# Row sums loaded, inverted and sent over three quads, and a third quad with five sum terms

## The chip, the cores and the metric

The kernel runs on one core of one Trainium2 chip. A core has a matrix engine (TensorE, PE in the profile; PEld is its weight load), a vector engine (VectorE, DVE), an activation engine (ScalarE, ACT), GpSimd (POOL) and SyncE (SP), which here issues nearly all DMA transfers. Each engine takes its own instructions in order and waits for semaphores. The metric is the device time of one execution in microseconds (us); the median of the runs is compared. A profile shows one execution: its span runs from the first to the last instruction.

## What is computed

Attention with normalised queries and keys, and then a feed-forward block whose activation is a softmax times its own input:

```python
# q, k, v: (8, 12, 448, 64)
q_n, k_n = rmsnorm(q, g_q), rmsnorm(k, g_k)
attn = softmax(q_n @ k_n.T / sqrt(64))          # rows divided by their sum
x = (attn @ v) -> (8 * 448, 12 * 64)            # 3584 tokens of 768
h = x @ w_in                                    # 768 -> 1024
solu = h * softmax(h)
out = layer_norm(solu) * g_ln @ w_out           # 1024 -> 768
```

The kernel doesn't divide the attention weights. It forms the exponentials, multiplies them by v, sums the exponentials of each row apart, and multiplies the result by the inverse of the sum only when the feed-forward block takes x in.

## The kernel before

**Stages.** The attention runs over 24 quads, numbered 0 to 23; a quad is four heads of one batch, so three quads make a batch of twelve heads. In the profile it takes the first 306.6 us. Then the feed-forward block runs in two stages, and PE works through them to the end at 789.4 us.

**A quad.** Quads 2 to 23 have one shape. The loop over m (lines 1573 to 1746) writes the order of all engines out by hand. The 448 keys are cut into seven groups (0 to 6) of 64. For each group PE forms the scores (`both_scores`, line 885), ScalarE takes the exponential into a tile E (line 845), and PE multiplies E by v into `o` (`both_values`, line 897). PE's order in a quad is scores 0, 1, 2, 3, values 0, scores 4, values 1, scores 5, values 2, scores 6, values 3 to 6. `o` is one PSUM tile with one buffer. `take` (line 1000, VectorE) copies it to `xo`, and values 0 of the next quad can't start before that copy has ended. The store of `xo` to DRAM is SP's (line 1009).

**Row sums.** The exponentials of a row are summed on PE by matmuls with a tile of ones (`sums`, line 962). To have fewer such matmuls, VectorE first adds E tiles in pairs: `add_pair` (line 905) makes a term of two tiles, `add_to` (line 911) adds a third to a term, `join_terms` (line 915) makes one of two terms. `quads[m]["terms"]` lists what the sums of quad m go over, in this order, with E6 put in front. A quad of `two_terms` ends with two terms, other late quads with three, quads 1 and 2 with four. The sums of three quads are formed together at the end of quads 2, 5, 8, 11, 14, 17, 20 and 23 (`sums_at`), 8 matmuls for each term.

**What becomes of the sums.** In the quad after, ScalarE copies them out of PSUM (`keep_sums`, lines 974 and 976) and SP sends them to DRAM (`sd`, line 979). Then, for batch b: `load_sums` (line 988) loads the batch's sums from DRAM spread over 128 partitions, 42 on each, into the tile `inv`, which has one buffer; `invert` (line 992) is VectorE's reciprocal; `send_inverses` (line 995) sends the inverses to DRAM (`rd`), from where the feed-forward stage loads them (`load_r`, line 1049) and multiplies x by them (`scale`, line 1062). The dictionary `inverts_at` (line 1471) says when: at its key m, SP loads at the start of quad m, VectorE inverts in the middle of the same quad, and SP sends at the start of quad m+1. Batch 7 is handled later, in the feed-forward stage.

**VectorE's order in a quad** (from quad 6 on): the take of the quad before, with the two or three short steps of the norm (lines 724 to 729) before or behind it; two row reductions of squares (line 696); two transposes of queries and keys (line 756), which wait for `qkn` from GpSimd (line 735); the reciprocal, where there is one; two pair adds, two further adds, the join, and in quads of `steps_at` two operations of the weight conversion (lines 545 and 546).

**SP's order in a quad:** load v (line 675), two stores of x (line 1009, behind the take), sums to DRAM, inverses to DRAM, load of sums, a load of weights (line 513), and the pieces of q and k (line 647, eight a quad from quad 6 on, ten before that), which ScalarE squares a quad and more later (line 690).

Of the kernel before, what the change touches and what calls it, by code (L numbers as in the profile page):

```python
# [366 lines left out]
def fast_path(  # L367
# [24 lines left out]
    nc = tc.nc  # L392
    B, H, S, D = q.shape
# [6 lines left out]
    NQ = B * NP // 2  # L400
# [225 lines left out]
    quads = {}  # L626
# [275 lines left out]
    def add_pair(m, x, y):  # L902
        d = quads[m]
        e = work.tile([P, 2, S], FP32, tag="es", name="es", bufs=6)
        nc.vector.tensor_tensor(e, d["E", x], d["E", y], OP.add)  # L905
        d.setdefault("terms", []).append((2, e))

    def add_to(m, k, x, engine):
        d = quads[m]
        e = d["terms"][k][1]  # L910
        engine.tensor_tensor(e, e, d["E", x], OP.add)  # L911
# [82 lines left out]
    def send_inverses(b):  # L994
        nc.sync.dma_start(rd[b].rearrange("j r c -> (j r c)").rearrange("(p x) -> p x", p=P), inverses[b])

    def take(m):
        d = quads[m]
        d["xo"] = work.tile([P, 2, S], FP32, tag="xo", name="xo", bufs=1)
        nc.vector.tensor_copy(d["xo"], d["o"][:, :, 0:S])  # L1000
        for i in range(2):
            del st[2 * m + i]
# [465 lines left out]
    combines_at[23] = (10, 11)  # L1468
    two_terms = (3, 4, 6, 7, 9, 10, 12, 13, 15, 16, 18, 19, 22)
    sums_at = (2, 5) + tuple(range(8, NQ, 3))  # L1470
    inverts_at = {4: (0,), 8: (1,), 10: (2,), 14: (3,), 16: (4,), 20: (5,), 22: (6,)}
    wq += [(moe_w_out, c + k, i) for c in range(HF) for k in (0, HF) for i in range(2)]
    again = [(w, w.shape[0] // P, i) for w in (moe_w_in, moe_w_out) for i in range(-(-w.shape[0] // P * w.shape[1] // S))]
    extent = consts.tile([P, len(again)], FP32, name="extent")
# [29 lines left out]
    with tc.manual_schedule():  # L1504
# [68 lines left out]
        for m in range(1, NQ):  # L1573
            a, b = 2 * m, 2 * m + 1
            next1 = m + 1 < NQ
            next2 = m + 2 < NQ
            early = EARLY <= m
            four = m < 3

            def score(x):  # L1580
                unit(lambda: both_scores(m, x))

            def value(x):
                unit(lambda: both_values(m, x))

            if m == 3:
                norm_gain()
            sent = None
            if kept:
                sent = keep_sums(*kept)  # L1590
                kept = None
            if next1:
                load_v(m + 1)
            beside = combines_at.get(m, ())
            if beside:
                if m - 1 in steps_at:
                    step = wq[steps_at.index(m - 1)]
                    pass_on(w_in[(0, 3, 1, 2)[step[1] // HD * 2 + step[2]]][0:1, step[1] % HD, 0:1])
                else:
                    pass_on(quads[m - 1]["terms"][-1][1][0:1, 0, 0:1])  # L1600
                for x in beside:
                    combine_in(x)
                take(m - 1)
            if early and next1:
                rsqrt_step(norms[m + 1])
            if m > 1 and not beside:
                take(m - 1)
            store_x(m - 1)
            if sent:
                sent()  # L1610
            for x in inverts_at.get(m - 1, ()):
                send_inverses(x)
            for x in inverts_at.get(m, ()):
                load_sums(x)
            if early and m + 2 in steps_at:
                load_next()
            if m == 1:
                score(0)
                score(1)
                score(2)  # L1620
                rsqrt_seed(norms[2])
                rsqrt_step(norms[2])
                normalise(4)
                normalise(5)
                load_pieces(8)
                score(3)
                squares(6)
                row_sums(6)
                qk_transpose(4)
                value(0)  # L1630
                score(4)
                squares(7)
                qk_transpose(5)
                row_sums(7)
                value(1)
                score(5)
                fold_sums(3)
                value(2)
                score(6)
                gains(2)  # L1640
            else:
                if m == 2:
                    add_pair(1, 0, 1)
                    add_to(1, 1, 2, nc.vector)
                    score(0)
                    rsqrt_seed(norms[3])
                if next1:
                    if not early:
                        rsqrt_step(norms[m + 1])
                    if m == 2:  # L1650
                        add_pair(1, 3, 4)
                        quads[1]["terms"].append((2, quads[1]["E", 5]))
                    normalise(a + 2)
                    normalise(b + 2)
                    if m == 22:
                        combine_in(9)
                if early:
                    load_pieces(2)
                else:
                    load_pieces(10)  # L1660
                    if m + 2 in steps_at:
                        load_next()
                if early and next2:
                    row_sums(a + 4)
                    row_sums(b + 4)
                    load_pieces(6)
                if m == NQ - 1:
                    scale(0)
                if m != 2:
                    score(0)  # L1670
                if m > 2 and not early:
                    squares(a + 4)
                    row_sums(a + 4)
                score(1)
                if next1:
                    qk_transpose(a + 2)
                if m > 2 and not early:
                    squares(b + 4)
                    row_sums(b + 4)
                if m == 2:  # L1680
                    score(2)
                    squares(a + 4)
                    row_sums(a + 4)
                    score(3)
                    squares(b + 4)
                    row_sums(b + 4)
                    qk_transpose(b + 2)
                else:
                    if next1:
                        qk_transpose(b + 2)  # L1690
                    for x in inverts_at.get(m, ()):
                        invert(x)
                    score(2)
                    score(3)
                if next2:
                    fold_sums(m + 2)
                value(0)
                score(4)
                if m in steps_at:
                    low_bits, join, product = convert_w(wq[steps_at.index(m)], raws[steps_at.index(m)])  # L1700
                    low_bits[0]()
                value(1)
                score(5)
                if m in steps_at:
                    low_bits[1]()
                if next1 and early and m not in sums_at:
                    gains(m + 1)
                add_pair(m, 0, 1)
                if four:
                    add_to(m, 0, 2, nc.vector)  # L1710
                    add_pair(m, 3, 4)
                else:
                    add_pair(m, 2, 3)
                    add_to(m, 0, 4, nc.vector)
                    add_to(m, 1, 5, nc.vector)
                    if m in two_terms:
                        join_terms(m)
                value(2)
                score(6)
                if next1 and (not early or m in sums_at):  # L1720
                    gains(m + 1)
                if m in steps_at:
                    join()
                if next2:
                    rsqrt_seed(norms[m + 2], m not in steps_at or m + 1 in steps_at)
                if m + 1 >= EARLY and m + 3 < NQ:
                    squares(a + 6)
                    squares(b + 6)
                if four:
                    quads[m]["terms"].append((2, quads[m]["E", 5]))  # L1730
            quads[m].setdefault("terms", []).insert(0, (2, quads[m]["E", NK - 1]))
            if m == NQ - 2:
                load_x(0)
                load_r(0)
            if m == NQ - 1:
                load_x(1)
                sizes(0)
                block_sums(0, 0)
                block_sums(0, 1)
            for x in range(3, NK):  # L1740
                value(x)
            waiting.append(m)
            if m in sums_at:
                unit(lambda: None)
                kept = end_sums()
                waiting.clear()
        take(NQ - 1)
        sent = keep_sums(*kept)
        store_x(NQ - 1)
# [185 lines left out]
```

## Time and profile before

| | |
|---|---|
| runs | 791.09 us median of 3 (790.87 to 793.43) |
| the profiled execution | 791.04 us, span 789.4 us |
| granted TensorE clock | 0.997 |
| PE, PEld busy | 769.7 us (97%), 473.1 us (60%) |
| DVE, ACT, POOL busy | 610.2 us (77%), 511.8 us (65%), 483.3 us (61%) |
| DMA | 134.27 MB, mean 170 GB/s |
| end of the attention's sums on PE | 306.55 us |

Busy time is the union of an engine's instructions; a matmul's end is modelled, so a busy PE is not a PE at its peak. In a row of the timeline the first two numbers are the start (us from the span's start) and the length of one or several like instructions; the bracket at its end is the idle time of that engine just before it and what ended it. In a row of waits stand the waiting instruction, what it waited for, the us in total, how often, and the longest. In a row of windows stand the window, its length, the busy time of each engine with its instructions in brackets (PE, PEld, DVE, ACT, POOL), the clock, the mean busy share of the 16 DMA engines and GB/s. The length of a row can overlap the start of the next, since an engine begins an instruction before the last has been acknowledged.

### The profile page before, as it was taken

What the parts mean: (1) busy time and instruction counts of PE and PEld (TensorE: products, weight loads), DVE (VectorE), ACT (ScalarE), POOL (GpSimd) and SP (SyncE); (2) the same over time, 40 slices, a digit from 0 to 9 for tenths busy, and PEclk for the clock granted to TensorE, in tenths of its full rate; (3) what the DMA queues carried; (4) which work ended last, traced back from release to release, by engine and by line L of the source; (5) the groups of instructions that cost most, each with busy time, mean ns of one, the idle gap of its engine ahead of it and who ended that gap; (6) DMA issues with size and microseconds to landing.
All of it is one profiled execution on the core that took longest, in us unless ns stands there. A gap on an engine that the chain in (4) does not pass through costs nothing.

```text
span 789.4 us, 14850 instructions
## 1 busy us (share of the span) xinstructions
PE 769.7 (97%) x5158; PEld 473.1 (60%) x5158; DVE 610.2 (77%) x1038; ACT 511.8 (65%) x847; POOL 483.3 (61%) x635
## 2 busy tenths in 40 slices
PE   8999998999999999999999999999999999999996
PEld 4444444444444444444444444444899999999996
DVE  6779989998999886677788667676697695776844
ACT  6778997878888873687777656556626445464410
POOL 2464443453544544454587688888898777777851
PEclk9999999999999999999999999999999999999998
DMA  9999999999999546677887777773757647457212
GB/s 161 180 178 198 192 202 159 202 183 171 182 181 187 127 129 155 162 182 174 197 186 168 165 156 168 160 184 75 216 157 248 201 147 253 149 179 249 99 55 86
DMA packets 279818, 134.27 MB, mean 170 GB/s; under 512 B 190324, under 2 KB 264884, under 8 KB 279732
## 3 DMA queue, kind: packets, MB, share of 16 engines
q1 hardware_dynamic: 265892, 123.31, 69.9%
q10 hardware_dynamic: 13840, 9.90, 4.3%
q8 instruction: 43, 0.70, 0.4%
q14 instruction: 43, 0.35, 0.2%
HBM read 96.12 MB, written 37.04 MB: 169 GB/s over the span
## 4 chain that ended last, share of the span: by engine, by line
PE 72%; DVE 10%; SPq 5%; issue 5%; DMA 4%; POOL 3%; ACT 1%; DVEq 0%
PE A L1340 16%; PE A L1114 14%; PE B L1114 9%; PE B L1340 8%; PE D L1114 5%; PE C L1114 5%; PE o L897 4%; PE C L1340 4%; SPq L647 4%; PE s L885 4%; POOL qkn L735 3%; DVE xo L1000 2%; DVE es L905 2%; DVE qkT L756 2%; DVE es L911 2%
## 5 line engine op out<-in xcount | busy, mean ns | idle before, releaser
L845 ACT ACTIVATE E<-s 128x896 f32<-128x896 f32 x144 | 124.4, 920 | 27.7 <-PE s L885 26.9
L885 PE MATMUL s<-qkT 64*64 64x448 f32 x1288 | 138.8, 540 | 0.0
L897 PE MATMUL o<-E,v 64*64 64x448 f32 x1104 | 120.8, 538 | 6.4 <-DVE xo L1000 6.4
L735 POOL TENSOR_TENSOR qkn<-qk,ny 128x896 f32<-128x896 f32 x45 | 77.1, 1735 | 74.5 <-DVE ny L729 42.0
L885 PEld LDWEIGHTS s<-qkT 64*64 64x64 f32 x1288 | 66.0, 190 | 59.2 <-issue 37.5
L897 PEld LDWEIGHTS o<-E,v 64*64 64x64 f32 x1104 | 41.1, 133 | 65.8 <-issue 45.1
L1340 PE MATMUL A<-w_out,sums 128*128 128x192 f32 x392 | 79.7, 326 | 0.0
L1340 PE MATMUL B<-w_out,sums 128*128 128x192 f32 x392 | 79.7, 326 | 0.0
L1114 PE MATMUL A<-w_in,xg 128*128 128x512 f32 x168 | 76.8, 593 | 0.0
L1114 PE MATMUL B<-w_in,xsum 128*128 128x512 f32 x168 | 76.7, 592 | 0.0
L1340 PEld LDWEIGHTS B<-w_out,sums 128*128 128x128 f32 x392 | 66.3, 190 | 0.0
L1340 PEld LDWEIGHTS A<-w_out,sums 128*128 128x128 f32 x392 | 66.3, 190 | 0.0
L756 DVE STREAM_TRANSPOSE qkT<-qkn 128x896 f32<-128x896 f32 x46 | 49.9, 1099 | 9.9 <-POOL qkn L735 9.9
L1114 PEld LDWEIGHTS B<-w_in,xsum 128*128 128x128 f32 x168 | 31.9, 190 | 40.2 <-issue 39.7
L1114 PEld LDWEIGHTS A<-w_in,xg 128*128 128x128 f32 x168 | 31.8, 190 | 40.1 <-issue 38.9
L1216 ACT ACTIVATE u<-u,shift,he 128x1024 f32<-128x1024 f32 x28 | 34.8, 1242 | 28.2 <-POOL shift L1212 28.1
L696 DVE TENSOR_REDUCE part<-sq 128x28 f32<-128x896 f32 x46 | 47.9, 1074 | 4.3 <-ACT sq L690 4.3
L905 DVE TENSOR_TENSOR es<-E 128x896 f32<-128x896 f32 x46 | 49.0, 1101 | 0.0
L1090 POOL TENSOR_TENSOR xsum<-xg 128x384 f32<-128x384 f32 x14 | 14.4, 1030 | 55.7 <-ACT xsum L1073 38.7
L911 DVE TENSOR_TENSOR es<-es,E 128x896 f32<-128x896 f32 x44 | 47.7, 1123 | 0.1
L1340 PE MATMUL A<-w_out,s 128*128 128x192 f32 x224 | 45.6, 326 | 0.0
L690 ACT ACTIVATE sq<-qk 128x896 f32<-128x896 f32 x45 | 41.0, 944 | 1.8 <-issue 0.6
(175 smaller groups left out, 1655.8 us busy)
## 6 DMA issues: line engine op xcount, KB each, us to landing
ur<-ud SPq DMA_DIRECT2D x60, 256.0 KB, 4.5
ud<-ub SPq DMA_DIRECT2D x112, 128.0 KB, 2.9
xd<-xo SPq DMA_DIRECT2D x48, 224.0 KB, 3.8
qk<-in_q_dram SPq DMA_DIRECT2D x92, 112.0 KB, 4.5
qk<-in_k_dram SPq DMA_DIRECT2D x92, 112.0 KB, 4.0
v<-in_v_dram SPq DMA_DIRECT2D x23, 448.0 KB, 5.2
out_dram<-P SPq DMA_DIRECT2D x19, 384.0 KB, 3.8
raw<-in_moe_w_in_dram SPq DMA_DIRECT2D x12, 512.0 KB, 5.4
```

Source lines behind the costliest of these rows:

```text
L690: nc.scalar.activation(d["sq"].rearrange("p (s b) d -> p s (b d)", s=2), d["qk"], AF.Square)
L696: nc.vector.tensor_reduce(norms[m]["part"][:, i], st[n]["sq"], AX, OP.add)
L735: e.tensor_tensor(d["qkn"].rearrange("p (s b) d -> p s b d", s=2), d["qk"].rearrange("p s (b d) -> p s b d", d=32), y.rearrange("p (s b) - ...
L756: nc.vector.transpose(d["qkT"].rearrange("p s t -> p (s t)"), d["qkn"].rearrange("p b d -> p (b d)"))
L845: nc.scalar.activation(e, s[:, :, 0:S], AF.Exp)
L885: nc.tensor.matmul(s[i * D : (i + 1) * D, h, 0:S], qkT[hh, i, 1, keys], qkT[hh, i, 0], start=True, stop=True)
L897: nc.tensor.matmul(d["o"][h * D : (h + 1) * D, i, 0:S], d["v"][pp, h, kc], d["E", kc][pp, h], start=kc == 0, stop=kc == NK - 1,)
L905: nc.vector.tensor_tensor(e, d["E", x], d["E", y], OP.add)
L911: engine.tensor_tensor(e, e, d["E", x], OP.add)
L1114: nc.tensor.matmul(k[bank], a[:, c], w_in[i][:, c], start=begin and c == 0, stop=c == HD - 1, skip_group_check=not begin,)
L1216: nc.scalar.activation(d["u"], d["u"], AF.Identity, scale=d["e"], bias=d["shift"])
L1340: nc.tensor.matmul(k[bank], a[:, c].rearrange("p a i -> p (a i)"), w_out[:, area, i, c], start=begin and c == 0, stop=c == KC - 1, skip_gr ...
```

## The change

Four edits. The table `inverts_at` becomes regular: batch x is loaded at the start of quad 4+3x (4, 7, 10, 13, 16, 19, 22 in place of 4, 8, 10, 14, 16, 20, 22). VectorE inverts it one quad after the load, in quad 5+3x, and SP sends the inverses at the start of quad 6+3x; for batch 6 that is behind the last quad. So each of the three steps has a quad of its own, and the reciprocals now stand in quads 5, 8, 11, 14, 17, 20 and 23.

In quad 2 (index 2, the third) E2 is no longer added to the first pair. The terms become E6, E5, E2, E0+E1, E3+E4 in this order, five in place of four (E6, E0+E1+E2, E3+E4, E5).

The third item of the change's title, two terms in the fifth quad, has no line in the diff: `two_terms` holds index 4 before and after.

```diff
-    inverts_at = {4: (0,), 8: (1,), 10: (2,), 14: (3,), 16: (4,), 20: (5,), 22: (6,)}
+    inverts_at = {4 + 3 * x: (x,) for x in range(B - 1)}
...
-            for x in inverts_at.get(m - 1, ()):
+            for x in inverts_at.get(m - 2, ()):
                 send_inverses(x)
             for x in inverts_at.get(m, ()):
                 load_sums(x)
...
-                    for x in inverts_at.get(m, ()):
+                    for x in inverts_at.get(m - 1, ()):
                         invert(x)
                     score(2)
                     score(3)
...
                 add_pair(m, 0, 1)
                 if four:
-                    add_to(m, 0, 2, nc.vector)
                     add_pair(m, 3, 4)
+                    quads[m]["terms"] = [(2, quads[m]["E", x]) for x in (5, 2)] + quads[m]["terms"]
...
-                if four:
-                    quads[m]["terms"].append((2, quads[m]["E", 5]))
             quads[m].setdefault("terms", []).insert(0, (2, quads[m]["E", NK - 1]))
...
+        for x in inverts_at.get(NQ - 2, ()):
+            send_inverses(x)
         take(NQ - 1)
```

## The prediction

> **What bounds the kernel now.** I read the page first, then the waits of TensorE (PE) and VectorE (DVE), then the rows of the tile `inv`, then the time of each quad from one `take` to the next. From the page:
>
> ```profile
> span 789.4 us, 14850 instructions
> PE 769.7 (97%) x5158; PEld 473.1 (60%) x5158; DVE 610.2 (77%) x1038; ACT 511.8 (65%) x847; POOL 483.3 (61%) x635
> ```
>
> PE looks full, but 19.7 us of the span are not, and the waits from quad 8 to quad 23 (110.6 to 295.8 us) all name DVE first; the waits of DVE over the same quads follow:
>
> ```profile
> PE o L897 <- DVE xo L1000: 5.9, 7, 1.5
> PE sm L962 <- DVE es L911: 2.9, 5, 1.2
> ...
> DVE inv L992 <- DMA inv<-sd: 8.6, 5, 3.7
> DVE qkT L756 <- POOL qkn L735: 6.0, 10, 1.8
> ```
>
> The same view names no wait of PE after 300 us, so whatever attention saves reaches the end. The tile `inv` holds the row sums; its load, and three of the five waits in DVE's timeline (start, us, instruction, idle before):
>
> ```profile
> L988 SPq DMA_DIRECT2D inv<-sd x8: 422/682/1317, 65.5 to 317.6; - x8
> ...
> 118.24 0.42 DVE L992 RECIPROCAL inv<-inv 128x42 f32<-128x42 f32 x1 [3.68 <-DMA inv<-sd]
> ...
> 142.40 0.42 DVE L992 RECIPROCAL inv<-inv 128x42 f32<-128x42 f32 x1 [1.03 <-DMA inv<-sd]
> ...
> 265.18 0.42 DVE L992 RECIPROCAL inv<-inv 128x42 f32<-128x42 f32 x1 [1.25 <-DMA inv<-sd]
> ```
>
> The reader is to see an instruction of 0.42 us that holds up its whole engine for a load issued in the same quad. Is DVE idle time worth anything? Windows from one take to the next, quads 8 to 13, and the whole of quads 8 to 22 (length, then PE, PEld, DVE, ACT, POOL busy):
>
> ```profile
> 109.48:124.22 14.74, 13.11 (x164) 5.98 (x160) 10.99 (x15) 10.65 (x17) 4.55 (x7) 1.00 1.06 190
> 124.22:136.29 12.07, 12.07 (x132) 5.77 (x132) 11.93 (x16) 11.51 (x16) 4.55 (x7) 1.00 0.84 150
> 136.29:147.80 11.51, 11.07 (x120) 4.98 (x112) 10.45 (x12) 9.87 (x15) 4.55 (x7) 1.00 1.01 203
> 147.80:159.61 11.81, 11.05 (x146) 5.22 (x144) 11.28 (x14) 8.91 (x14) 6.79 (x9) 1.00 1.08 185
> ...
> 109.48:294.57 185.09, 176.33 (x1972) 82.73 (x1968) 169.15 (x203) 151.78 (x215) 85.86 (x119) 1.00 0.89 171
> ```
>
> Against them the start of the first `values` matmul of a quad, which needs the take before it, and the start of the sums of quad 8, from PE's timeline:
>
> ```profile
> 110.71 0.93 PE L897 MATMUL o<-E,v 64*64 64x448 f32 x8
> 118.34 0.59 PE L962 MATMUL sm<-El,ones 128*32 128x224 f32 x8
> ...
> 148.94 0.98 PE L897 MATMUL o<-E,v 64*64 64x448 f32 x8 [0.76 <-DVE xo L1000]
> 162.52 0.93 PE L897 MATMUL o<-E,v 64*64 64x448 f32 x8
> ...
> 273.22 0.93 PE L897 MATMUL o<-E,v 64*64 64x448 f32 x8
> 283.75 0.95 PE L897 MATMUL o<-E,v 64*64 64x448 f32 x8
> 295.71 0.98 PE L897 MATMUL o<-E,v 64*64 64x448 f32 x8 [0.50 <-DVE xo L1000]
> ```
>
> Four constants come out. PE undisturbed takes 283.75-273.22 = **10.53** per quad, and 162.52-148.94 = **13.58** in a quad that ends with sums. The first value follows a take's start by at least 148.94-147.80 = **1.14**. The values end 118.34-110.71 = **7.63** after the first. From 110.71 to 295.71 PE needs 10 x 10.53 + 5 x 13.58 = 173.2 of 185.0 us: 11.8 idle. DVE over the same quads has 185.09 us, of which 8.6 are the wait for `inv`: 176.5 left. So **DVE paces these quads**, PE is 3.3 us behind it as second, and DVE's wait is worth nearly its length.
>
> **The change, part by part.** (1) Loads move from quads 8, 14, 20 to 7, 13, 19; inverses to 5, 8, 11, 14, 17, 20, 23 (before: 4, 8, 10, 14, 16, 20, 22); sends to 6, 9, 12, 15, 18, 21 and behind the last quad. Every inverse now stands a whole quad, 10 us and more, behind its load; the longest of the five waits is 3.7, so all 8.6 us should go. Behind the waiting reciprocal stood es adds, the join, the weight conversion and the take, and PE waited for the adds (2.9) and the takes (5.9).
>
> What is late next? I walk the quads, with take(m) the later of DVE's own work and the values' end. Quad 8: DVE needs 14.74-3.68 = 11.06, take(8) at 120.54; first value of 9 at 110.71+13.58 = 124.29 (PE, above 121.68). Quad 9: 12.07 more, take(9) at 132.61; values end 131.92, so no wait. First value of 10: 134.82 by PE, 133.75 by DVE. Quad 10: 11.51 less its wait of 1.03 and less a reciprocal, 0.34 (0.42 less the 0.08 by which the end of one row overlaps the start of the next, as at 47.58+1.09 and 48.59 below): 10.14, take(10) at 142.75; values end 142.45. Margin 0.3, the least of all. Quad 11: 11.81+0.34, take(11) at 154.90. Further on DVE leads nowhere but lags, so its sum holds: 185.09-8.6-0.34 (six reciprocals become five) = 176.1, still above PE's 173.2. **Gain of this part: 9.0 us.** Its bounds: 11.8 if PE alone counted; 2.9 if only PE's waits at the sums went and the takes stayed late.
>
> (2) Quad 2 adds one term to the sums and drops one DVE add. DVE and PE there, and DVE's next wait:
>
> ```profile
> 47.58 1.09 DVE L911 TENSOR_TENSOR es<-es,E 128x896 f32<-128x896 f32 x1
> 48.59 1.19 DVE L905 TENSOR_TENSOR es<-E 128x896 f32<-128x896 f32 x1
> 53.78 1.08 DVE L696 TENSOR_REDUCE part<-sq 128x28 f32<-128x896 f32 x1 [2.63 <-ACT sq L690]
> ...
> 49.83 0.59 PE L962 MATMUL sm<-es,ones 128*32 128x224 f32 x8 [0.52 <-DVE es L905]
> 50.24 0.56 PE L962 MATMUL sm<-E,ones 128*32 128x224 f32 x8
> 50.73 0.22 PE L479 MATMUL pg<-ident,grow 8*128 8x8 f32 x1
> ```
>
> The add of 1.09 goes, so the second pair ends near 48.7 instead of 49.8. A term is about 0.4 on PE (50.24-49.83). With the ready terms E6, E5, E2 first (from 48.10), nine terms end near 50.1 where eight ended at 50.7: PE gains **0.6**, bounds -0.4 (the term with no wait saved) and 0.9 (the wait twice over). DVE's 1.09 is not gained: its next reduction waits 2.63 for ScalarE's squares, which stand behind exponentials of PE's scores, so DVE too moves by 0.6. In quads 4 and 5 one reciprocal leaves and one comes: nothing.
>
> (3) "Two terms in the fifth": `two_terms` already holds index 4 and no line of the diff touches it. Zero.
>
> (4) Quad 23 gets a reciprocal between `scale(0)` and its pairs:
>
> ```profile
> 301.63 3.69 DVE L911 TENSOR_TENSOR es<-es,E 128x896 f32<-128x896 f32 x2
> ...
> 305.68 0.94 PE L962 MATMUL sm<-es,ones 128*32 128x224 f32 x16
> ```
>
> Its last add ends at 305.32 and the last term starts about 0.4 after 305.68, so 0.7 of cover; the reciprocal takes 0.34 to 0.42: **0**, or 0.4 with the cover gone. The send after the loop goes to an SP that only waits for the last store.
>
> (5) SP's queue: the counts stay, but six issues of 0.7 move into quads 6, 7, 12, 13, 18, 19. SP's stores of x and loads of v that begin and end two rotations of three quads:
>
> ```profile
> 125.33 1.24 SPq L1009 DMA_DIRECT2D xd<-xo  x2
> 157.77 0.86 SPq L675 DMA_DIRECT2D v<-in_v_dram  x1
> 160.72 1.24 SPq L1009 DMA_DIRECT2D xd<-xo  x2
> ...
> 198.34 1.24 SPq L1009 DMA_DIRECT2D xd<-xo  x2
> 232.52 1.74 SPq L675 DMA_DIRECT2D v<-in_v_dram  x1
> ```
>
> Quads 9 to 11 hold SP 33.3 us, quads 15 to 17 35.9, less a send of 0.7 that leaves, 35.2. DVE afterwards needs 12.07+10.14+12.15 = 34.4 and in the mean 176.1/5 = 35.2 for three quads. It fits, barely, so I charge nothing and keep it as a rival; charged in full it would be 6 x 0.7 = 4.2.
>
> The Trainium skill (Perfetto Trace Analysis, What "DMA-bound" means) counts a kernel as DMA-bound when the issuing engine's sequencer track is solid DMA slices. By that rule SP would set quads 9 to 19, and the time would be that of the first or second rival below. The trace agrees in part only: SP ends its work of quad 11 at 158.6 and has nothing to do until the store at 160.72.
>
> Sum: 9.0+0.6 = 9.6 against the profiled run's own 791.04 us (span 789.4 and 1.6 around it; the median shown is 791.09). I keep 0.5 back for the two margins of 0.3: gain 9.1, **781.9 us**. Its own range is 781.0 (nothing kept back, 0.9 in quad 2) to 784.5 (five of DVE's ten waits for POOL, 0.6 each, grow to twice their length as DVE comes earlier: 3.0).
>
> **The rivals.**
>
> ```profile
> 86.50:107.90 21.40, 21.40 (x228) 10.09 (x232) 21.23 (x27) 19.56 (x29) 9.09 (x14) 1.00 1.11 208
> 107.90:256.10 148.20, 140.36 (x1572) 65.75 (x1571) 136.99 (x165) 123.88 (x176) 67.13 (x96) 1.00 0.99 181
> ```
>
> *DMA takes the bound's place* (7%). The DMA share is 0.99 over quads 8 to 19. If that is full, these quads cannot shrink; left are quad 20's wait of 1.25, 0.34 in quad 22 and 0.6: gain 2.2, 788.8 us. Against it: quads 6 and 7 ran at share 1.11 and 208 GB/s, and the new pace needs 181 x 148.2/(148.2-7.4) = 190, the 7.4 being the waits without quad 20's.
>
> *SP paces, slower* (4%). If SP's order sets when the squares run, the six issues put into its full quads cost those 4.2 and only 2.2 are gained: 793.0 us. It decides once loads land behind the squares. In quad 14 that is:
>
> ```profile
> 182.07 3.46 SPq L647 DMA_DIRECT2D qk<-in_k_dram  x4
> 192.32 1.79 ACT L690 ACTIVATE sq<-qk 128x896 f32<-128x896 f32 x2
> DMA to landing us min/median/max: 3.3/4.0/6.1
> ```
>
> The last piece is issued near 185.0 and lands near 189, 3 us ahead of its use; SP would have to fall 3 us behind.
>
> *Only the sums' waits go* (12%): DVE's saved time turns into waits for E or for POOL's `qkn`, and the takes come as late as now. Gain 2.9+0.6 = 3.5, 787.5 us. For it: 6.0 us of DVE waits for POOL already. Against it: the walk finds DVE late, not early, from quad 11 on.
>
> *The inverses still wait* (2%), for instance through a dependence on the whole of `sd`: 0.6 gained, 790.4 us.
>
> **How the numbers follow.** The forecast has 75%, the rivals 25%. The range begins at 780.0, half way from 781.4 to PE's bound (791.04-11.8-0.6 = 778.6), and ends at 787.0, near the third case; about 2 in 10 lie outside. A change of under 0.3% (2.4 us) cannot be told from none here. Faster is the forecast, the third case and 2 of DMA's 7: 0.89; same is the other 5 and the waiting inverses: 0.07; slower 0.04.
>
> **What would show it.** No wait of a reciprocal for `inv<-sd`; quad 8 from take to take near 11 us; the stretch from first value 8 to first value 23 near 176 instead of 185.0; PE's waits at the sums gone, and about 3 us (176.1-173.2) of waits for the take left; sums of quad 2 without a wait. I am wrong if squares or `qkn` wait for loads, or if ScalarE's exponentials begin to hold PE.

## The result, and the profile after

The changed kernel takes 780.13 us (median of 4 runs, 779.79 to 780.71), the kernel before, timed beside it, 790.98 us (4 runs, 790.21 to 793.43): a ratio of 0.9858 [0.9836, 0.9881]. The forecast was 781.9 us. The ratio applied to the median that the prediction started from gives 791.09 x 0.9858 = 779.9, which is 0.1 below the range given (780.0 to 787.0); both 779.9 and 780.13 lie below the likeliest case's own range (781.0 to 784.5). So the sign and most of the size were right, but more was gained than the forecast allowed for: 10.71 us between the two profiled executions, where 9.1 were forecast. Two executions of the experiments below ran at a much lower granted clock, one of the changed kernel (1163.49 us, clock 0.655) and one of the kernel before with four small matmuls (1016.1 us, 0.754), and stand in no median or ratio. The profiled execution of the changed kernel took 780.33 us. From its page:

```profile
span 778.4 us, 14869 instructions
PE 768.0 (99%) x5166; PEld 474.9 (61%) x5166; DVE 611.4 (79%) x1037; ACT 512.4 (66%) x847; POOL 481.5 (62%) x635
```

TensorE (PE) is busy about as long as before (768.0 against 769.7) in a span that is 11.0 us shorter. So 9.3 of the 11.0 are idle time of PE that is gone. The waits of PE from 36 to 310 us, and those of VectorE (DVE) from 110 to 286 us, which is quad 8 to quad 23:

```profile
PE o L897 <- DVE xo L1000: 2.3, 4, 0.9
...
DVE qkT L756 <- POOL qkn L735: 6.0, 10, 1.8
```

The 8.6 us of waits for `inv` are gone without a rest, and so are PE's waits at the sums (2.9). Of its 5.9 us of waits for the take from quad 8 to quad 23, 2.05 are left: 0.89, 0.86 and 0.30; the fourth wait of the 2.3, 0.28 us at 75.12, lies ahead of quad 8. What DVE waits for GpSimd is what it was, 6.0 in ten places: the waits did not move there. The time of quads 8 to 11 and of quads 8 to 22, from one take to the next (columns as before: window, length, PE, PEld, DVE, ACT, POOL busy, clock, DMA share, GB/s):

```profile
108.87:119.84 10.97, 10.97 (x142) 5.23 (x138) 10.90 (x16) 9.88 (x15) 4.56 (x7) 1.00 1.01 186
119.84:131.93 12.09, 12.09 (x140) 5.81 (x136) 11.95 (x16) 10.60 (x16) 4.56 (x7) 1.00 1.09 196
131.93:142.03 10.10, 10.10 (x112) 4.69 (x108) 10.06 (x11) 9.14 (x14) 4.56 (x7) 1.00 0.95 217
142.03:154.05 12.02, 12.02 (x152) 5.79 (x148) 11.49 (x16) 11.29 (x16) 5.99 (x9) 1.00 1.00 183
...
108.87:284.71 175.84, 174.10 (x1972) 83.52 (x1968) 168.49 (x201) 151.66 (x215) 84.37 (x119) 1.00 0.91 181
```

DVE's busy time in the long window hardly changed (169.15 before, 168.49 now), while the window went from 185.09 to 175.84. PE's rows at the points that the prediction used, from its timeline:

```profile
50.12 0.22 PE L479 MATMUL pg<-ident,grow 8*128 8x8 f32 x1
...
110.10 0.93 PE L897 MATMUL o<-E,v 64*64 64x448 f32 x8
...
204.49 0.98 PE L897 MATMUL o<-E,v 64*64 64x448 f32 x8 [0.89 <-DVE xo L1000]
...
285.85 0.98 PE L897 MATMUL o<-E,v 64*64 64x448 f32 x8 [0.30 <-DVE xo L1000]
...
296.69 0.70 PE L1114 MATMUL A<-w_in,xg 128*128 128x512 f32 x1
...
771.94 0.81 PE L1340 MATMUL B<-w_out,sums 128*128 128x192 f32 x4
```

The same two rows of the kernel before, where the feed-forward block begins and where PE's last matmuls are:

```profile
306.55 0.70 PE L1114 MATMUL A<-w_in,xg 128*128 128x512 f32 x1
...
781.64 0.81 PE L1340 MATMUL B<-w_out,sums 128*128 128x192 f32 x4
```

These rows divide the difference of the two profiled executions, 791.04 - 780.33 = 10.71 us. The attention ends 306.55 - 296.69 = 9.86 earlier. PE's feed-forward part is 0.16 longer (476.06 against 475.90, counted to the end of the last row). From PE's last matmul to the end of the span it was 789.4 - 782.45 = 6.95 and is 778.4 - 772.75 = 5.65, so 1.30 less. Around the span it is 1.93 in place of 1.64, so 0.29 more. 9.86 + 1.30 - 0.16 - 0.29 = 10.71.

### The profile page after: what moved, and what is told of

It reads as the page before. It is cut to its first block, busy times and chain, and to the rows that moved or that the text cites. A ratio compares the mean times of both kernels' runs of the same rounds, so it can differ in the third digit from the quotient of the medians.

```text
span 778.4 us, 14869 instructions
## 1 busy us (share of the span) xinstructions
PE 768.0 (99%) x5166; PEld 474.9 (61%) x5166; DVE 611.4 (79%) x1037; ACT 512.4 (66%) x847; POOL 481.5 (62%) x635
## 4 chain that ended last, share of the span: by engine, by line
PE 90%; SPq 3%; DMA 2%; DVE 2%; ACT 1%; issue 1%; POOL 0%; DVEq 0%
PE A L1340 16%; PE A L1114 14%; PE o L897 12%; PE s L885 12%; PE B L1114 9%; PE B L1340 8%; PE D L1114 5%; PE C L1114 5%; PE C L1340 4%; PE sm L962 3%; SPq L647 2%; PE pt L799 1%; DVE xo L1000 1%; DMA qk<-in_k_dram 1%; ACT E L845 1%
## 5 line engine op out<-in xcount | busy, mean ns | idle before, releaser
L845 ACT ACTIVATE E<-s 128x896 f32<-128x896 f32 x144 | 124.5, 920 | 22.3 <-PE s L885 21.5
```

Source lines behind the costliest of these rows:

```text
L845: nc.scalar.activation(e, s[:, :, 0:S], AF.Exp)
```

## The experiments

The theory: DVE paces quads 8 to 22, each microsecond that its reciprocal waits for `inv` costs one, and quad 2 adds 0.6. The rivals under test are those of the prediction, SP and DMA above all, and a question that the result raised, the 1.30 us behind the last matmul. Ratios are against runs of the kernel before made beside each experiment.

**The inverses alone.** The regular table with its places in the loop and the send behind the loop, without the edit of quad 2:

```diff
-    inverts_at = {4: (0,), 8: (1,), 10: (2,), 14: (3,), 16: (4,), 20: (5,), 22: (6,)}
+    inverts_at = {4 + 3 * x: (x,) for x in range(B - 1)}
...
-            for x in inverts_at.get(m - 1, ()):
+            for x in inverts_at.get(m - 2, ()):
...
-                    for x in inverts_at.get(m, ()):
+                    for x in inverts_at.get(m - 1, ()):
...
+        for x in inverts_at.get(NQ - 2, ()):
+            send_inverses(x)
```

> The first part alone: the new table of loads, inverses and sends, with the sum terms of quad 2 as before. Theory (VectorE paces quads 8 to 22, and its waits for the inverses were on that path): no reciprocal waits, the stretch from take(7) to take(22) is 176 us instead of 185.1, and the attention ends 9.0 us earlier. Rival (only the waits of PE at the sums go): 3 us earlier. A second question is the last semaphore of PE, which came 1.3 us behind those of the other engines in the profile of before and with them in the profile of the changed kernel. If that hangs on the number of PE instructions (here as before), it is late here too and the time is 782.0; if it was chance, it may come on time and the time is 780.7 to 782.0.

Measured: 781.71 us (781.23 to 782.1), the kernel before 792.21 beside it, ratio 0.9873 [0.9848, 0.9899]. The first take in DVE's timeline, PE's timeline at the end of the attention, and PE's waits:

```profile
27.37 1.08 DVE L1000 COPY xo<-o 128x896 f32<-128x896 f32 x1
...
297.68 2.84 PE L1114 MATMUL A<-w_in,xg 128*128 128x512 f32 x6
...
PE o L897 <- DVE xo L1000: 2.3, 4, 0.9
PE sm L962 <- DVE es L905: 0.5, 1, 0.5
```

No group of waits for `inv` is left in it. In the kernel before, the first take is this row:

```profile
27.00 1.08 DVE L1000 COPY xo<-o 128x896 f32<-128x896 f32 x1
```

This execution began 0.37 later, so its attention is better counted from the first take: 297.68 - 27.37 = 270.31 us, where the kernel before needed 306.55 - 27.00 = 279.55. The inverses carry 9.24, and the changed kernel, which began at 27.01 and needed 269.68, has 0.63 more, the terms. Of PE's waits for the sums one is left, 0.5 in quad 2, the one that the other part takes away.

**The terms alone.** Only the edit of quad 2:

```diff
                 if four:
-                    add_to(m, 0, 2, nc.vector)
                     add_pair(m, 3, 4)
+                    quads[m]["terms"] = [(2, quads[m]["E", x]) for x in (5, 2)] + quads[m]["terms"]
...
-                if four:
-                    quads[m]["terms"].append((2, quads[m]["E", 5]))
```

> The second part alone: five sum terms in quad 2, the table of inverses as before. Theory: quad 3 begins 0.6 us earlier on PE and the attention ends 0.6 earlier; the five waits for the inverses stay at 8.6 us in all. Time 790.4 if the last semaphore of PE is late as before; 789.1 if that semaphore hangs on the number of PE instructions (8 more here) and comes on time. Rival: the 0.6 is eaten by the wait in quad 8, whose load is issued by SP whatever PE does: 791.0.

Measured: 790.86 us (788.04 to 792.64), ratio 0.9976 [0.9955, 0.9996]. In its profile the waits for `inv` are longer than in that of the kernel before. Here are the group of waits, the load and the reciprocal of quad 8, quad 2's end and the end of the attention:

```profile
DVE inv L992 <- DMA inv<-sd: 11.6, 5, 6.2
...
50.21 0.22 PE L479 MATMUL pg<-ident,grow 8*128 8x8 f32 x1
...
116.39 0.66 SPq L988 DMA_DIRECT2D inv<-sd  x1
...
120.18 0.42 DVE L992 RECIPROCAL inv<-inv 128x42 f32<-128x42 f32 x1 [6.15 <-DMA inv<-sd]
...
309.08 2.84 PE L1114 MATMUL A<-w_in,xg 128*128 128x512 f32 x6
```

Quad 2 ends 0.52 earlier than before (50.73), and yet the attention ends 2.53 later. SP issued the load 1.74 later than in the kernel before (114.65), and quad 8's wait is 2.47 longer (6.15 against 3.68). The edit of quad 2 touches neither that load nor that reciprocal. So I take the wait to vary from one execution to the next, and its size in one profile to be one sample; that is argued, since no kernel with these waits was profiled twice. The ratio's interval leaves 0.3 to 3.6 us for the edit; the trace shows 0.5, and the comparison above 0.63.

**Three loads earlier, inverses where they were.** In the old kernel the loads of quads 8, 14 and 20 are issued one quad earlier:

```diff
+    loads_at = {4: (0,), 7: (1,), 10: (2,), 13: (3,), 16: (4,), 19: (5,), 22: (6,)}
...
-            for x in inverts_at.get(m, ()):
+            for x in loads_at.get(m, ()):
                 load_sums(x)
```

> Before, with nothing but the loads of batches 1, 3 and 5 a quad earlier (quads 7, 13, 19); every inverse and send stays where it was, so the reciprocals of quads 10 and 16 still wait for a load of their own quad. Theory: the waits in quads 8, 14 and 20 (3.68, 1.89, 1.25) go and come out of the time in full, 6.8 us: 784.2. What is left of the change's gain then belongs to the waits of quads 10 and 16 (1.03 and 0.76) and to a reciprocal less in quad 22. Rival (only PE's waits at the sums): 2.9 us, 788.1. Rival (the loads of SP's full quads 7, 13 and 19 push q and k back): no gain or slower.

Measured: 788.53 us (786.07 to 790.67), ratio 0.996 [0.9941, 0.998]: a miss, 4.3 us above what was expected, of which 1.2 are the base (792.21 where 791.04 had been taken). The group of waits, DVE's rows in quads 10, 14, 16 and 20, and the end of the attention:

```profile
DVE inv L992 <- DMA inv<-sd: 4.9, 3, 2.7
...
140.45 0.42 DVE L992 RECIPROCAL inv<-inv 128x42 f32<-128x42 f32 x1 [2.70 <-DMA inv<-sd]
...
187.70 0.37 DVE L992 RECIPROCAL inv<-inv 128x42 f32<-128x42 f32 x1
...
213.83 0.42 DVE L992 RECIPROCAL inv<-inv 128x42 f32<-128x42 f32 x1 [1.88 <-DMA inv<-sd]
...
261.06 0.38 DVE L992 RECIPROCAL inv<-inv 128x42 f32<-128x42 f32 x1
...
302.41 2.84 PE L1114 MATMUL A<-w_in,xg 128*128 128x512 f32 x6
```

Quad 16's row in the kernel before:

```profile
216.62 0.42 DVE L992 RECIPROCAL inv<-inv 128x42 f32<-128x42 f32 x1 [0.76 <-DMA inv<-sd]
```

The three waits whose loads moved are gone, but quad 10's grew from 1.03 to 2.70 and quad 16's from 0.76 to 1.88. I had taken each wait as a fixed sum. It is the lead of DVE over SP's load, plus the time that the load takes. In quad 10 DVE is ready 3.62 us earlier than before, about the wait of 3.68 that fell away in quad 8; SP issues the load only 2.44 earlier (136.28 against 138.72), and from the issue to the reciprocal it is 4.17 in place of 3.68. In quad 16 DVE is 3.91 earlier, SP's load 3.53, and from issue to reciprocal it is 4.17 in place of 3.43, so there most of the growth is the load itself. What is left is 4.9 (the third one, of 0.3, is in quad 4), so 3.7 fewer, and the attention ends 4.14 earlier.

**The load ahead of the store.** In the old kernel the same-quad load goes in front of the two stores of x on SP, with inverses and their quads unchanged:

```diff
+            for x in inverts_at.get(m, ()):
+                load_sums(x)
             store_x(m - 1)
             if sent:
                 sent()
...
-            for x in inverts_at.get(m, ()):
-                load_sums(x)
```

> Before, with the load of sums put ahead of the two stores of x on SP's queue, in the same quad as ever; table, inverses, sends and terms as before. In the profile of before the load stands behind stores that wait for the take; SP is through with v at 112.1, 137.2, 186.2, 211.6 and 260.05 in quads 8, 10, 14, 16 and 20 and issues the load at 114.65, 138.72, 187.57, 213.19 and 261.43. Theory: the length of a wait is set by when SP comes to the load; the five waits shrink by 2.5, 1.5, 1.4, 1.6 and 1.4 (those of quads 10, 16 and 20 to nothing), from 8.6 to 1 to 2 us, and the attention ends as much earlier: 7 us, 784 to 785. Rival (a wait is set by how long the load takes to land): they stay, 791.

Measured: 786.11 us (784.27 to 787.94), ratio 0.9906 [0.988, 0.9932]; 1 to 2 us above what was expected; its profiled execution was the longest of its runs, 787.94. The group of waits, the rows of quads 8 and 20, and the end of the attention:

```profile
DVE inv L992 <- DMA inv<-sd: 4.9, 3, 3.9
...
115.01 0.47 SPq L988 DMA_DIRECT2D inv<-sd  x1
...
118.26 0.42 DVE L992 RECIPROCAL inv<-inv 128x42 f32<-128x42 f32 x1 [3.85 <-DMA inv<-sd]
...
257.21 0.47 SPq L988 DMA_DIRECT2D inv<-sd  x1
...
261.46 0.37 DVE L992 RECIPROCAL inv<-inv 128x42 f32<-128x42 f32 x1
...
302.83 2.84 PE L1114 MATMUL A<-w_in,xg 128*128 128x512 f32 x6
```

Where SP is in time, going ahead of the store is enough (quad 20: a load 4.25 ahead, no wait; quad 14 has none either). Quads 10 and 16, expected without a wait, keep 0.69 and 0.39. In quad 8 SP itself arrives late, at 115.01, and the wait stays. A load in the same quad as its use depends on SP's backlog; no reciprocal whose load stood a quad earlier waited in any of the profiles.

**What a microsecond of wait costs.** The profiled executions, from the first take to the start of the feed-forward block, with the kernel before with four small matmuls that is told further down:

| kernel | first take, feed-forward | length, us | shorter by | waits for `inv`, us | waits fewer by |
|---|---|---|---|---|---|
| before | 27.00, 306.55 | 279.55 | | 8.6 | |
| load ahead of the store | 26.81, 302.83 | 276.02 | 3.53 | 4.9 | 3.7 |
| three loads earlier | 26.81, 302.41 | 275.60 | 3.95 | 4.9 | 3.7 |
| inverses alone | 27.37, 297.68 | 270.31 | 9.24 | 0 | 8.6 |
| terms alone, with its 0.52 put back | 27.00, 309.08 | 282.60 | -3.05 | 11.6 | -3.0 |
| four small matmuls | 27.96, 309.61 | 281.65 | -2.10 | 10.6 | -2.0 |

The columns "shorter by" and "waits fewer by" agree within 0.3 us, on both sides of the kernel before, but for the inverses alone, with 0.6 more; 0.34 of that is what the prediction charged for the sixth reciprocal that no longer stands in quads 8 to 22. So DVE's wait costs its whole length. The old kernel's time is also unsteady: beside the first experiment its runs lay between 788.9 and 795.3 us, those of the inverses alone within 0.9 us. The changed kernel, run again, stayed between 779.98 and 781.32 (it had been expected within 1 us of 780.1), and in its second profile no reciprocal waits either. That the waits make the old kernel's spread fits these runs, but is not shown.

**Is SP or DMA the bound now?** Two kernels built on the changed one. The first has one more load of 21.5 KB on SP in each of quads 8 to 19, of data that nobody uses:

```diff
+            if 8 <= m < 20:
+                extra = small.tile([P, 42], FP32, tag="extra", name="extra", bufs=1)
+                nc.sync.dma_start(extra, v[0, 0].rearrange("s d -> (s d)")[0 : P * 42].rearrange("(p x) -> p x", p=P))
```

> The changed kernel with one more small load on SP's queue in each of the quads 8 to 19, of the shape of the load of sums, into a tile that nobody reads: 12 issues of about 0.7, 8.4 us of SP's time. In the changed kernel's profile SP has no pause over 0.1 us from quad 7 to 17 and stands 1.2 to 4.7 us behind the takes. Theory (VectorE paces, SP only follows with 3 us of lead left): the lead is used up, then SP decides: 784 to 785. Rival (SP paces already): all of it comes on top, 788.5. Rival (SP has slack that its rows do not show): 780.1.

The second has no loads of v from quad 9 on:

```diff
+        if m >= 9:
+            d["v"] = quads[m - 1]["v"]
+            return
```

> The changed kernel without the loads of v for quads 9 to 23, which use the v of quad 8; the attention's values are therefore not the reference's. That takes 0.5 to 0.9 us of SP's time and 448 KB of DMA out of every quad. Theory (VectorE paces): the takes stay where they are and the time is 780.1, within 0.5. Rival (SP or the DMA engines pace the changed kernel): up to 12 x 0.7 = 8 us faster; PE's own need allows 2.6 of it, 777.5.

Measured: 781.56 us (781.21 to 781.81), ratio 0.9863 [0.9835, 0.9891], with twelve issues more, and 781.99 us (781.78 to 782.7), ratio 0.9871 [0.9844, 0.9899], with fifteen loads fewer. The changed kernel itself, run again beside them, took 780.24, ratio 0.9851 [0.9827, 0.9875]. First the kernel with more issues, in the groups of SP, the timeline of PE and its last matmuls:

```profile
L1617 SPq DMA_DIRECT2D extra<-in_v_dram x12: 426/652/1017, 114.4 to 243.7; - x12
...
296.52 2.84 PE L1114 MATMUL A<-w_in,xg 128*128 128x512 f32 x6
...
771.77 0.81 PE L1340 MATMUL B<-w_out,sums 128*128 128x192 f32 x4
```

Twelve issues with a median of 0.65 us, some 8 us on a queue that looked full, and the attention ends at 296.52 against 296.69: nothing. I had expected 784 to 785, so this is a miss. In quads 8 to 19 the rows of SP add up to 130.2 us where they were 129.6 in the changed kernel, and a piece of q or k took 0.90 us in the mean (95 pieces) in place of 0.98 (97). I read this as issue times that give way, but what sets them is not shown: without the loads of v, where SP has pauses, the mean was 0.91. The time of the kernel with more issues is longer only behind the last matmul (the span is 779.7, and 779.7 - 772.58 = 7.12). Then the kernel without the loads of v, its end of attention and, from the timeline, SP at the end of quad 11:

```profile
149.72 2.60 SPq L647 DMA_DIRECT2D qk<-in_k_dram  x3
155.53 1.24 SPq L1012 DMA_DIRECT2D xd<-xo  x2
...
297.02 2.84 PE L1117 MATMUL A<-w_in,xg 128*128 128x512 f32 x6
```

SP now stands idle for 3.2 us ahead of that store (152.32 to 155.53), and the attention ends no earlier (its first take is at 27.21, 0.20 later than in the changed kernel, its end 0.33 later). Over quads 8 to 19 the DMA share fell from 1.00 to 0.93. The takes stayed, as expected, but the time did not: it is 1.9 us above the 780.1 that was expected within 0.5. Neither SP's issues nor what DMA moves sets the pace of the changed kernel's attention. SP's track in the changed kernel, between quads 10 and 11, shows no such pause, only one of 0.44 us ahead of the store:

```profile
138.51 4.89 SPq L647 DMA_DIRECT2D qk<-in_q_dram  x4
143.45 3.34 SPq L647 DMA_DIRECT2D qk<-in_k_dram  x4
146.89 0.48 SPq L675 DMA_DIRECT2D v<-in_v_dram  x1
147.81 1.24 SPq L1009 DMA_DIRECT2D xd<-xo  x2
```

So a track with hardly a gap was no proof of a bound. By the rule of the Trainium skill (Perfetto Trace Analysis, What "DMA-bound" means) a solid track of the issuing engine is one of the signs of one. These two runs do not agree with it here: the attention ended at 296.52 and 297.02 against 296.69.

**The time behind the last matmul.** In the kernel before and in the one with the inverses alone, both with 5158 PE instructions, PE's last semaphore instruction came 1.3 and 0.9 us after those of the other engines; in the changed kernel, with 5166, it came with them. These are the rows of the last line of the kernel, for PE's queue and VectorE's before, and for PE's queue after (the second time is the start of the last one):

```profile
L1930 PEldq EVENT_SEMAPHORE  x2: 51/51/51, 787.5 to 789.4; - x2
L1930 DVEq EVENT_SEMAPHORE  x2: 21/21/21, 787.5 to 788.0; - x2
...
L1930 PEldq EVENT_SEMAPHORE  x2: 51/51/51, 777.8 to 778.4; - x2
```

To see whether the count matters by itself, four matmuls of 16 columns were put ahead of the warm-up, first in the kernel before, then in the one with the inverses alone:

```diff
+        for _ in range(4):
+            nc.tensor.matmul(o[:, 0:16], w[:, 0:P], w[:, 0:16], start=True, stop=True)
```

> Before, with four matmuls of 16 columns put ahead of the five that warm PE up, which is 8 PE instructions more, as many as the change adds; nothing else. They write what the next matmul overwrites. If the late last semaphore of PE hangs on the number or place of PE's instructions, it comes with the other engines' here and the time is 789.7; if it is chance or hangs on something else, the time is 791.0 and the semaphore may be late or not.

> The inverses alone, and four matmuls of 16 columns ahead of the warm-up, so that PE has as many instructions as in the changed kernel. In the profiles so far the last semaphore of PE came 0.9 to 1.3 us behind those of the other engines in the three kernels with 5158 PE instructions and with them in the three with 5166. Theory: it comes on time here, and the time is 0.9 us below that of the inverses alone, 780.8. Rival (it goes by the moved sends or the terms): it is late, 781.7.

Measured: 792.67 us (790.4 to 794.55), ratio 1.0009 [0.9991, 1.0028], and 782.07 us (781.04 to 782.88), ratio 0.9865 [0.9837, 0.9893]. Neither is faster than its base. The tail did shrink in both, to 791.0 - 785.51 = 5.49 and 781.1 - 775.40 = 5.70, but in the first the waits for `inv` were 10.6 and the first take came 0.96 later than in its base, and in the second it came 1.80 later. What the shorter tail is worth in the time is therefore not shown by these two. The time behind the last matmul in all profiles (span, less start and length of the last row):

| PE instructions | kernels | span's end behind the last matmul, us |
|---|---|---|
| 5158 | before, inverses alone, three loads earlier, load ahead of the store | 6.95, 6.70, 6.54, 7.43 |
| 5166 and 5182 | after, after again, terms alone, the two with four small matmuls, the one told next | 5.65, 5.55, 5.52, 5.49, 5.70, 5.69 |
| 5166 | one more issue, no loads of v | 7.12, 6.93 |

The first two rows fit a count, the third does not. In the third row the last semaphore instructions of all engines come together, and late: with one more issue VectorE's first semaphore instruction of the last line comes 6.5 us behind the last matmul, where it is 5.1 in the changed kernel; without the loads of v it comes after 5.1 too, but PE's last instruction of the type DRAIN starts at 779.8, 1.3 behind the last of the other engines. So the tail takes about 5.6 or 6.5 to 7.4 us with the same work at the end, and what decides between them stays open. It accounts for most of the 1.3 and 1.8 us by which the two kernels of the third row are slower than the changed one. What lies around the span does follow the count in every run: a run's time less its span is 1.6 to 1.7 us with 5158 PE instructions, 1.75 to 2.0 with more.

**Three terms in quads 15 and 18.** PE still waits for the take in four places of the changed kernel, most of all at the start of quad 16 (0.89 us, in the row at 204.49 above), behind quads in which DVE makes two sum terms. Quads 15 and 18 get three terms, so DVE saves a join in each and PE has eight matmuls more for each:

```diff
-    two_terms = (3, 4, 6, 7, 9, 10, 12, 13, 15, 16, 18, 19, 22)
+    two_terms = (3, 4, 6, 7, 9, 10, 12, 13, 16, 19, 22)
```

> The changed kernel with quads 15 and 18 taken out of the quads that join their terms, so that each ends with three terms in place of two. In the changed kernel PE still waits 0.89 and 0.86 us for the takes of these two quads, the longest of VectorE's rotation (join and weight conversion). VectorE loses an add of 1.09 in each, PE gains a term of 0.38 in each. Theory: the waits in quads 16 and 19 go, PE sets the pace there, and the attention ends 2 x (0.87-0.38) = 1.0 us earlier: 779.2. Rival (SP sets the pace once VectorE is faster): the takes come no earlier, and the two terms make it 0.8 us slower: 780.9.

Measured: 778.39 us (777.95 to 780.21), ratio 0.9842 [0.9823, 0.9861]. PE's waits and the end of the attention:

```profile
PE o L897 <- DVE xo L1000: 0.3, 1, 0.3
...
294.91 2.84 PE L1114 MATMUL A<-w_in,xg 128*128 128x512 f32 x6
```

The attention ends 1.78 us earlier than in the changed kernel, more than the 1.0 expected; the waits shown fell by 2.0. It was not timed beside the changed kernel, and the two ratios' intervals overlap, so the order of the two rests on the traces and on medians taken at different times. With 0.3 us of PE's waits left, hardly more is to be had from DVE in these quads; that is argued from the row of waits, not tried.

## What the prediction had right, and the step that failed

**What bounds the kernel: right.** "DVE paces these quads, PE is 3.3 us behind it as second, and DVE's wait is worth nearly its length" is what the table of waits shows, in steps from -3.0 to 8.6 us. That the waits of PE "all name DVE first" leaves out one: the same view has a wait of 0.5 us for ScalarE's exponentials, which is gone too.

**The walk over the quads: right to 0.3 us.** With the 0.6 of quad 2 taken off, it gave the takes of quads 8 to 11 at 119.94, 132.01, 142.15 and 154.30; they came at 119.84, 131.93, 142.03 and 154.05. From the first value of quad 8 to that of quad 23 it gave 176.0 (185.0 less 9.0); the rows give 285.85 - 110.10 = 175.75.

**Part (2): right.** Quad 2 ended at 50.12, 0.61 before the 50.73 of before, against 0.6. The sums wait no more:

```profile
48.50 0.94 PE L962 MATMUL sm<-E,ones 128*32 128x224 f32 x16
49.25 0.94 PE L962 MATMUL sm<-es,ones 128*32 128x224 f32 x16
```

DVE's next reduction still waits for ScalarE, 2.90 where it was 2.63, as the prediction had argued when it did not count the add of 1.09 as gained:

```profile
53.18 1.09 DVE L696 TENSOR_REDUCE part<-sq 128x28 f32<-128x896 f32 x1 [2.90 <-ACT sq L690]
```

**Parts (3) to (5), at nothing: right.** The reciprocal in quad 23 cost nothing: from the first value of quad 23 to the feed-forward's start it is 10.84 both before and after. SP at nothing was right for a stronger reason than the one given. "It fits, barely" compared issue times summed from one trace with DVE's pace, as if they were fixed; with twelve issues more the others were shorter, and the attention ended no later.

**The step that failed: the sum behind the attention.** The forecast adds up the gain in the attention and takes all that lies behind it as fixed: "whatever attention saves reaches the end". That sentence was right, but it also put the time behind PE's last matmul at nothing without a reason, since a PE without waits after 300 us says nothing of what follows its last matmul. That time fell by 1.30 us. The feed-forward part (0.16) and the time around the span (0.29) went the other way, so 0.85 us were gained outside the attention, where the sum has no term. The range had no room for it either, since its lower end, 780.0, was worked out from the sum and from PE's bound, both of the attention alone. Why the end of the program became shorter stays open: in ten of the twelve profiles it goes with the number of PE instructions, in two it does not.

The second term that was off is the 0.5 "kept back for the two margins of 0.3". Neither margin became a wait: no take from quad 8 on waited for PE, and the reciprocal in quad 23 cost nothing. The sum without it, 9.6, was met to 0.26 (9.86). 0.85 + 0.5 + 0.26 are the 1.61 us between 10.71 and 9.1. One sum is off by a little: with nothing kept back and 0.9 in quad 2, 791.04 - 9.9 is 781.1, not 781.0.

Part of the close match is luck. The 8.6 us were read from one execution as if they were a property of the kernel, and the attention's gain is counted against that same execution. Two other profiles with the same five waits had 10.6 and 11.6, and beside the experiments the old kernel's median was 791.5 to 792.9; the gain is a difference against a moving number.

**The rivals.** *DMA takes the bound's place* and *SP paces* fell with the two runs on SP. The changed kernel also moved more over quads 8 to 19, which take 140.24 us from take to take in place of 147.99, than before (181 GB/s at a share of 0.99):

```profile
108.87:249.11 140.24, 138.50 (x1568) 66.08 (x1564) 136.41 (x163) 123.73 (x177) 65.62 (x96) 1.00 1.00 192
```

A share of 0.99 here was not a ceiling. *Only the sums' waits go* fell, since the stretch of quads 8 to 22 became 9.25 us shorter and DVE's waits for GpSimd stayed at 6.0. *The inverses still wait* fell with the list of waits.

**What would show it.** All signs came: no reciprocal waits, quad 8 takes 10.97, from the first value of quad 8 to that of quad 23 it is 175.75, PE's waits at the sums are gone, those of quad 2 too, and from quad 8 to quad 23 2.05 us of waits for the take are left where about 3 were forecast.

## What to carry to other kernels

When a small instruction on an in-order engine waits for a transfer issued shortly before on a busy queue, look first whether that engine paces its stage; if it does, the wait can cost its whole length, as it did here. Moving the use a quad behind the load took it away in every profile, while moving only some of the loads passed part of it on to the next. Take such a wait from several executions before pricing it: its size hangs on when each of the two queues arrives and on how long the transfer takes. Before an issue queue without gaps is called the bound, add issues to it and see whether the end moves.

## What the runs showed of the hardware

SP's issue times are not fixed. A piece of q, one of 92 of the same shape, took between 0.33 and 3.95 us to issue in the changed kernel (median 0.72), and twelve issues more within a queue that had hardly a gap left the end of the attention where it was (296.52 against 296.69). The end of the program takes 5.5 to 5.7 us behind the last matmul in some of the kernels and 6.5 to 7.4 in others; with 5158 PE instructions PE's last semaphore instruction is 0.9 to 1.8 us late, and with eight more it is not, but two kernels with 5166 end late all the same. The issue times of q are a row of the changed kernel's groups:

```profile
L647 SPq DMA_DIRECT2D qk<-in_q_dram x92: 327/722/3951, 4.3 to 245.3; - x92
```
